# Chunk-selected attention and a soft mixture of experts: score groups regrouped, weight loads moved between pairs, first output rows stored by column halves

## The chip, the cores and the metric

The kernel runs on one core of one Trainium2 chip. Its engines work side by side and wait for each other through semaphores: TensorE (PE in the profile, its weight loads PEld), VectorE (DVE), ScalarE (ACT), GpSimd (POOL) and SyncE (SP). 16 DMA engines move data between HBM and the on-chip memory SBUF; matmuls write to PSUM. The metric is the device time of one execution in microseconds (us), as the median of several runs.

## The reference

Attention over 4 images x 8 heads, 768 positions, 64 channels a head. Each query sees 6 of 24 chunks of 32 keys, chosen by an upper bound of its scores, and within them the causal part:

```python
ub = sum(maximum(q * k_min, q * k_max), axis=-1)      # per query and chunk
ub = where(causal, ub, -1e9)
top_chunks = argsort(ub)[..., -6:]
scores = where(selected & causal, q @ k.T / 8, -1e9)
attn = softmax(scores);  x = attn @ v                 # 3072 rows x 512
```

The result goes through a soft mixture of 8 experts with 4 slots each (32 slots):

```python
logits = x @ phi                                      # 3072 x 32
slot_in = softmax(logits, over rows of all images).T @ x
slot_out[e] = relu(slot_in[e] @ w1[e]) @ w2[e]        # w1 512x1024, w2 1024x512
out = softmax(logits, over slots) @ slot_out          # 3072 x 512, float32
```

The first softmax runs over all 3072 rows, so no expert can start before the attention of all images is done.

## The kernel before

Attention goes by **pairs** of heads: 16 pairs, four to an image. The main loop (L479 to L566) is one pass for each pair i, software-pipelined by hand: the order in which the code issues instructions is the order in which each engine runs them. A pass holds the score groups of pair i (`scores`, `expo`), the chunk choice of pair i+1 (`ubound`, `select`, `ns_transposes`), the transposes of keys and queries of pair i+2, the product with v of pair i-1 (`pv`), the normalisation and transposition of pair i-2, and the loads of k and q of pair i+4 and of v of pair i+2. After every fourth pair come the steps of the experts (`moe_...`).

**Score groups.** Keys are cut into six blocks of 128, and block kg is needed by query blocks kg to 5, which makes 21 blocks of 128 x 128 for a head. `GROUPS` packs them into six groups of 384 or 512 columns. A piece (kg, q0, w, c) is key block kg against w queries from its own diagonal plus q0, put at column c. Each piece takes one score matmul (L270) and one or two mask matmuls (L280) for each head. `expo` takes one exponential on ScalarE over both heads of a group (L293), and GpSimd zeroes the upper triangle of the first 128 columns (L295). Scores live in two PSUM buffers (`p_sc`), so a group's matmuls wait for the exponential two groups earlier. Groups 0 and 1 stand at the head of the pass, 2 and 3 after the key transposes and the first part of `pv`, 4 and 5 after the query transposes.

**Weights.** Sixteen expert weights, w_sb0 to w_sb7 for w1 and w_sb8 to w_sb15 for w2 (w0 to w15 in this text), are loaded by GpSimd's DMA queue with a conversion from float32 to bfloat16, 1 MB each as written. `wplan` says how many are issued in each pass (`weights`, L473): after the loads of v (L535), in the last two passes at the head (L483). k, q and v go through the same queue.

**Tail.** After the loop the last pair is finished, the logits of the last image are reduced (L605 to L637; `keep` issues dummy matmuls), and the experts follow: `experts_in` (w1) for two halves of the hidden units, `hidden_T` transposes, `experts_out(f, gs, ys)` (w2) for hidden half f, expert groups gs (group 0 uses w8 to w11, group 1 w12 to w15) and column halves ys of the output. `so_sb` is the slots' output, scaled by `zinv` (from `zsum`). `csums` sums the row weights with 24 matmuls for `cinv`. The last loop (L737) makes 24 blocks of 128 rows, two matmuls each, scaled on VectorE and ScalarE in turn, and stores them on SP's queue, two blocks to a DMA.

Of the kernel before, what the change touches and what calls it, by code (L numbers as in the profile page):

```python
# [10 lines left out]
F32 = mybir.dt.float32  # L11
BF16 = mybir.dt.bfloat16
ALU = mybir.AluOpType
ACT = mybir.ActivationFunctionType
# [6 lines left out]
NQT = 6  # L21
P = 128
# [5 lines left out]


GROUPS = [  # L30
    [(0, 0, 384, 0)],
    [(1, 0, 256, 0), (0, 384, 128, 256)],
    [(2, 0, 512, 0)],
    [(5, 0, 128, 0), (1, 256, 384, 128)],
    [(3, 0, 384, 0)],
    [(4, 0, 256, 0), (0, 512, 256, 256)],
]
WIDTH = [sum(p[2] for p in g) for g in GROUPS]
BLOCK = {}
for _g, _pieces in enumerate(GROUPS):  # L40
    for _kg, _q0, _w, _c in _pieces:
        for _x in range(0, _w, P):
            BLOCK[(_kg, _kg + (_q0 + _x) // P)] = (_g, _c + _x)


@with_exitstack
def kernel(
# [10 lines left out]
    nc = tc.nc  # L58
    B, H = q.shape[0], q.shape[1]
    scale = 1.0 / (D ** 0.5)  # L60
    NPB = H // 2
    NPAIR = B * NPB
    Dm, NS = moe_phi.shape
    E, F = moe_w1.shape[0], moe_w1.shape[2]
    SPE = NS // E
    NDG, NFG = Dm // P, F // P
    EARLY = 14
    LAST = NPAIR - 1

    ctx.enter_context(tc.manual_schedule())  # L70
    static = ctx.enter_context(tc.tile_pool(name="static", bufs=1))


    p_sc = ctx.enter_context(tc.tile_pool(name="p_sc", bufs=2, space=PSUM))
# [12 lines left out]
    si_acc = static.tile([P, NDG + 1, NS], F32, name="si_acc")  # L87
    m_run = [static.tile([P, NS], F32, name=f"m_run{i}") for i in range(2)]
    w_sb = []
    for i in range(EARLY):  # L90
        w_sb.append(static.tile([P, NDG * F], BF16, name=f"w_sb{i}"))
    identf = static.tile([P, P], F32, name="identf")
    ones_sq = static.tile([P, P], BF16, name="ones_sq")
    NJ = NQT // 2
# [168 lines left out]
    def scores(i, g):  # L263
        ps = p_sc.tile([P, 2, 512], F32, name="sc_ps", tag="sc")
        kT, qT, nsT = st["kT", i], st["qT", i], st["nsT", i]
        for kg, q0, w, c in GROUPS[g]:
            qs = slice(kg * P + q0, kg * P + q0 + w)
            for h in range(2):
                r = slice(h * 64, (h + 1) * 64)
                nc.tensor.matmul(  # L270
                    ps[:, h, c:c + w], lhsT=kT[r, kg * P:(kg + 1) * P], rhs=qT[r, qs],
                    start=True, stop=False,
                )
            t0, t1 = kg + q0 // P, kg + (q0 + w) // P
            runs = [(x, max(t0, x * NJ), min(t1, (x + 1) * NJ)) for x in range(2)]
            runs = [r for r in runs if r[1] < r[2]]
            for x, f, l in runs:
                for h in range(2):
                    r = slice(h * 64, (h + 1) * 64)
                    nc.tensor.matmul(  # L280
                        ps[:, h, c + (f - t0) * P:c + (l - t0) * P],
                        lhsT=smask[r, x, kg].rearrange("p a b -> p (a b)"),
                        rhs=nsT[r, (f - x * NJ) * P:(l - x * NJ) * P], start=False, stop=(l == t1),
                    )
        st["scps", i, g] = ps

    def expo(i, g):
        w = WIDTH[g]
        if w == 512:
            e = ep.tile([P, 2, 512], BF16, name="e_sb", tag="e_sb")  # L290
        else:
            e = ep3.tile([P, 2, 384], BF16, name="e3_sb", tag="e3_sb")
        nc.scalar.activation(e[:, :, :w], st.pop(("scps", i, g))[:, :, :w], func=ACT.Exp, scale=scale)  # L293

        nc.gpsimd.affine_select(  # L295
            out=e[:, :, :P], in_=e[:, :, :P], compare_op=ALU.is_ge, fill=0.0,
            base=0, pattern=[[0, 2], [1, P]], channel_multiplier=-1,
        )
        st["e", i, g] = e

    def pv(i, ts):
        if i == LAST and ts[0] == 0:
            st["at", i] = p_tp.tile([P, 2, 3 * (D + 1)], F32, name="at_ps", tag="tp")
        elif i == LAST and ts[0] == 3:
            st["at", i] = p_sc.tile([P, 2, 512], F32, name="at_ps", tag="sc")
        elif ts[0] == 0:
            st["at", i] = p_at.tile([P, 2, 512], F32, name="at_ps", tag="at")
        at, tb = st["at", i], 3 if i == LAST and ts[0] > 2 else 0
        for t in ts:
            for h in range(2):  # L310
                o = at[:, h, (t - tb) * (D + 1):(t - tb + 1) * (D + 1)]
                for kg in range(t + 1):
                    g, c = BLOCK[(kg, t)]
                    nc.tensor.matmul(  # L314
                        o, lhsT=st["e", i, g][:, h, c:c + P], rhs=v_t[i % NV][:, h, kg, :],
                        start=(kg == 0), stop=(kg == t),
                    )
# [147 lines left out]
            step(i // NPB)  # L465


    wplan = {i: 1 for i in range(-1, NPAIR)}
    for i in (0, 1):
        wplan[i] = 0  # L470
    nw = 1

    def weights(i):  # L473
# [97 lines left out]
    BL = B - 1  # L571
# [12 lines left out]
    def keep(n):  # L584
        for _ in range(n):
            nc.tensor.matmul(h_ps[0][:, 1, :], lhsT=ident, rhs=w_sb[0][:, :512], start=True, stop=True)
# [22 lines left out]
    nc.tensor.matmul(pmT[:, :P], lhsT=pm, rhs=identf, is_transpose=True)  # L609
    mneg = small.tile([NS, 1], F32, name="mb", tag="mb")  # L610
    nc.vector.tensor_reduce(mneg, pmT, axis=AX.X, op=ALU.max, negate=True)
    keep(2)
    rep = identf[:NS, :NS].rearrange("p (o s) -> p o s", o=1)
    nc.tensor.matmul(
        lg2, lhsT=mneg.broadcast_to([NS, P]), rhs=rep.broadcast_to([NS, NQT, NS]), start=False, stop=True,
# [7 lines left out]
    st["d", BL] = d_sb  # L623
    rm = small.tile([P, NQT, 1], F32, name="rm", tag="rm")
    nc.vector.tensor_reduce(rm, lg1, axis=AX.X, op=ALU.max)
    dm = small.tile([P, 1, NS], F32, name="dm", tag="dm")
    nc.vector.tensor_tensor(dm[:, 0, :], m_old, bc, op=ALU.add)
    nc.scalar.activation(dm, dm, func=ACT.Exp)
# [8 lines left out]
    keep(1)  # L637
    moe_dispatch(BL)

    op = ctx.enter_context(tc.tile_pool(name="op", bufs=5))  # L640
    si = st.pop("si")
    zrow = tail.tile([1, 4, CH], F32, name="zrow")
    nc.gpsimd.memset(zrow, 1.0)
# [7 lines left out]
    for g in range(2):  # L651
# [3 lines left out]
            si_acc[:1, NDG, sl].rearrange("p (j s) -> p j s", j=4),  # L655
            si[:1, NDG, sl].rearrange("p (j s) -> p j s", j=4), op=ALU.add,
        )
    cinv = tail.tile([P, B * NQT], F32, name="cinv")
    zinv = tail.tile([P, 1], F32, name="zinv")
    cT = cT_all.rearrange("p (m a) (c x) -> p m x (a c)", a=2, x=2)  # L660

    h_sb = tail.tile([P, 2, 512], BF16, name="h_sb")
# [22 lines left out]
            i_ = hT_ps.rearrange("p a (j s) -> p a j s", j=4)[:, :, :, g * SPE:(g + 1) * SPE]  # L685
            nc.vector.tensor_copy(o, i_)

    def zsum():
        ps = p_tp.tile([P, 1], F32, name="z_ps", tag="tp")
        nc.tensor.matmul(  # L690
            ps, lhsT=zrow.rearrange("p j s -> p (j s)"), rhs=identf[:1, :1], start=True, stop=True)
        nc.vector.reciprocal(zinv, ps)

    def csums():
        ps = p_tp.tile([P, B * NQT], F32, name="cs_ps", tag="tp")
        for n in range(B * NQT):
            nc.tensor.matmul(
                ps[:, n:n + 1], lhsT=cT[:, n // 2, n % 2], rhs=ones_sq[:, :1], start=True, stop=True)
        nc.vector.reciprocal(cinv, ps)

    HD = Dm // 2
    so_t = p_at.tile([P, 2, 512], F32, name="so_ps", tag="at")
    so_ps = [so_t[:, y, :HD] for y in range(2)]

    def experts_out(f, gs, ys):
        for y, g in ((y, g) for y in ys for g in gs):
# [14 lines left out]
    hidden_T(0)  # L721
    experts_in(1, 1)
    relu(1)
    experts_out(0, [0], [0, 1])
    hidden_T(1)
    zsum()
    experts_out(0, [1], [0, 1])
    experts_out(1, [0, 1], [0])
    nc.scalar.activation(so_sb[0], so_ps[0], func=ACT.Copy, scale=zinv)
    experts_out(1, [0, 1], [1])  # L730
    nc.scalar.activation(so_sb[1], so_ps[1], func=ACT.Copy, scale=zinv)
    csums()


    homes = ((p_sc, "sc"), (p_tp, "tp"), (p_sc, "sc"), (p_tp, "tp"), (p_at, "at"))
    n = 0
    for m in range(B * NQT // 2):  # L737
        o_sb = op.tile([P, 2, Dm], F32, name="o_sb", tag="o_sb")
        rows = out[m * 2 * P:(m + 1) * 2 * P, :].rearrange("(p x) d -> p x d", x=2)
        for x in range(2):  # L740
            pool, tag = homes[n % 5]
            if n == 0:
                o_ps = pool.tile([P, 2, Dm], F32, name="o2_ps", tag=tag)
                halves = [o_ps[:, y, :HD] for y in range(2)]
            else:
                o_ps = pool.tile([P, Dm], F32, name="o_ps", tag=tag)
                halves = [o_ps[:, y * HD:(y + 1) * HD] for y in range(2)]
            for y in range(2):
                nc.tensor.matmul(halves[y], lhsT=cT[:, m, x], rhs=so_sb[y], start=True, stop=True)  # L749
            if n == 0:  # L750
                for y in range(2):
                    nc.vector.tensor_scalar_mul(o_sb[:, x, y * HD:(y + 1) * HD], halves[y], cinv[:, n:n + 1])
            elif x == 0:
                nc.vector.tensor_scalar_mul(o_sb[:, x, :], o_ps, cinv[:, n:n + 1])
            else:
                nc.scalar.activation(o_sb[:, x, :], o_ps, func=ACT.Copy, scale=cinv[:, n:n + 1])  # L756
            n += 1
            if m in (0, B * NQT // 2 - 1):
                nc.sync.dma_start(out=rows[:, x], in_=o_sb[:, x, :])
        if m not in (0, B * NQT // 2 - 1):  # L760
            nc.sync.dma_start(out=rows, in_=o_sb)


# [28 lines left out]
```

## Time and profile before

| | |
|---|---|
| median of 3 runs | 171.62 us (171.58 to 172.8) |
| the profiled execution | 172.21 us, of which its span 170.5 us |
| busy share of the span | PE 81%, DVE 71%, ACT 72%, POOL 61% |
| loads (GpSimd's queue) | 38416 packets, 26.25 MB as written |
| stores (SP's queue) | 6.29 MB |
| weight loads | 16 of 1024 KB, median 14.4 us from issue to landing |

The span runs from the first instruction to the last of one execution, and all times in the text are counted from its start. A line of the rows in order of time has start and duration in us, engine, source line, operation, written tile and read tiles, shape and number of instructions; in brackets stands the idle time of the engine just before, and who ended it. A line of the windows has the stretch, its length, busy time of PE, PEld, DVE, ACT and POOL with the number of instructions, the granted TensorE clock (1 is full speed), the DMA share and GB/s. The slices cut the span into 40 parts of 4.26 us; a digit is a share in tenths. DMA shares can pass 1, since packets overlap.

### The profile page before, as it was taken

To read this page: it belongs to the slowest core of one execution; us is meant where nothing else is said; L and a number is where in the kernel's file an instruction comes from. 1 tells how busy PE (TensorE), PEld (TensorE's weight loads), DVE (VectorE), ACT (ScalarE), POOL (GpSimd) and SP (SyncE) were. 2 spreads that over 40 slices of the span, in tenths; PEclk is the share of its full clock that TensorE was granted. 3 is DMA by queue.
4 is the path that set the end of the run, shared out by engine and by line. 5 is a ranking of instruction groups with operands and counts; after the bars stand their busy time and mean duration, and the time that the engine had idled before them with its cause. 6 is when DMAs were issued, how large, how long until landed. Compare 5 with 4: busy or idle time off the path is not lost.

```text
span 170.5 us, 6183 instructions
## 1 busy us (share of the span) xinstructions
PE 137.8 (81%) x2574; PEld 99.3 (58%) x2575; DVE 121.5 (71%) x416; ACT 122.6 (72%) x166; POOL 104.0 (61%) x202
## 2 busy tenths in 40 slices
PE   0458988999999898999999899979889989896300
PEld 0335555777666767766776667657566855763200
DVE  3468768999999976999997798988742651166510
ACT  3355999999999877999987799978777522175510
POOL 7977759788878777888878878547663800000000
PEclk9999999999999999999999999999999999999965
DMA  3999999999999999999999999999999980029995
GB/s 46 163 156 185 182 212 188 129 152 184 184 214 190 211 197 209 193 211 195 212 197 205 196 207 202 203 203 200 202 208 212 215 163 13 4 76 407 404 400 195
DMA packets 40460, 32.94 MB, mean 193 GB/s; under 512 B 26352, under 2 KB 34544, under 8 KB 40432
## 3 DMA queue, kind: packets, MB, share of 16 engines
q0 software_dynamic: 38416, 26.25, 104.2%
q1 hardware_dynamic: 2016, 6.29, 9.4%
q8 instruction: 20, 0.33, 0.7%
q14 instruction: 8, 0.07, 0.1%
HBM read 52.49 MB, written 6.29 MB: 345 GB/s over the span
## 4 chain that ended last, share of the span: by engine, by line
PE 39%; ACT 21%; DVE 15%; DMA 14%; issue 5%; POOL 2%; DVEq 0%; ACTq 0%; POOLq 0%
ACT e_sb L293 15%; DMA k_in<-in_k_dram 10%; PE sc_ps L270 7%; PE at_ps L314 5%; PE tr_ps L181 5%; PE sc_ps L280 5%; DMA out_dram<-o_sb 4%; DVE x_sb L327 3%; PE h_ps L670 2%; PE so_ps L710 2%; DVE qpn L216 2%; PE ub_ps L229 2%; DVE mx L241 2%; ACT qT L190 2%; PE xT_ps L336 2%
## 5 line engine op out<-in xcount | busy, mean ns | idle before, releaser
L293 ACT ACTIVATE e_sb<-sc_ps 128x768 bf16<-128x768 f32 (+1 forms) x96 | 82.9, 930 | 9.7 <-PE sc_ps L280 9.7
L295 POOL TENSOR_SCALAR_AFFINE_SELECT e_sb<-e_sb 128x256 bf16<-128x256 bf16 x96 | 38.7, 413 | 19.6 <-ACT e_sb L293 18.9
L270 PE MATMUL sc_ps<-qT,kT 64*128 64x384 bf16 (+3 forms) x288 | 40.3, 299 | 4.2 <-ACT e_sb L293 4.1
L280 PE MATMUL sc_ps<-nsT,smask 64*128 64x384 bf16 (+2 forms) x320 | 38.6, 281 | 0.0
L314 PE MATMUL at_ps<-v_t,e_sb 128*128 128x65 bf16 x672 | 29.8, 194 | 1.5 <-DVE x_sb L327 1.2
L314 PEld LDWEIGHTS <-e_sb 128*128 128x128 bf16 x672 | 25.3, 98 | 3.9 <-DVE x_sb L327 1.2
L270 PEld LDWEIGHTS <-kT 64*128 64x128 bf16 x288 | 17.0, 95 | 15.5 <-issue 10.4
L241 DVE MAX8 mx<-ub_ps 128x8 f32<-128x8 f32 (+1 forms) x192 | 16.9, 161 | 3.6 <-PE ub_ps L229 2.0
L280 PEld LDWEIGHTS <-smask 64*128 64x128 bf16 x320 | 16.6, 96 | 3.8 <-issue 0.6
L199 DVE TENSOR_REDUCE mm<-kT 128x24 bf16<-128x768 bf16 x16 | 15.1, 945 | 4.6 <-ACT kT L190 4.5
L190 ACT COPY kT<-tr_ps 128x768 bf16<-128x768 bf16 x16 | 12.8, 799 | 7.5 <-PE tr_ps L181 6.7
L134 POOL DMA_DIRECT2D v_t<-in_v_dram x16 | 16.7, 1045 | 2.0 <-PE ns_ps L252 1.4
L327 DVE TENSOR_TENSOR x_sb<-at_ps,inv 128x768 bf16<-128x768 f32 (+1 forms) x17 | 15.5, 911 | 0.6
L205 DVE TENSOR_REDUCE mm<-kT 128x24 bf16<-128x768 bf16 x16 | 15.1, 943 | 0.0
L181 PE MATMUL tr_ps<-ident,k_in 128*64 128x128 bf16 x192 | 9.4, 240 | 6.3 <-DMA k_in<-in_k_dram 5.5
L190 ACT COPY qT<-tr_ps 128x768 bf16<-128x768 bf16 x16 | 12.9, 805 | 2.0 <-PE tr_ps L181 2.0
L129 POOL DMA_DIRECT2D k_in<-in_k_dram x16 | 11.7, 729 | 1.5 <-POOLq L776 0.8
L122 POOL DMA_DIRECT2D w_sb<-in_moe_w_dram x16 | 11.4, 710 | 1.5 <-DMA w_sb<-in_moe_w_dram 1.5
L756 ACT ACTIVATE o_sb<-o_ps,cinv 128x512 f32<-128x512 f32 x12 | 8.1, 686 | 4.9 <-PE o_ps L749 2.4
L129 POOL DMA_DIRECT2D q_in<-in_q_dram x16 | 11.5, 720 | 0.0
L216 DVE TENSOR_SCALAR qpn<-qT 128x768 bf16<-128x768 bf16 x16 | 11.0, 685 | 0.0
L347 DVE COPY xT_sb<-xT_ps 128x768 bf16<-128x768 bf16 (+1 forms) x15 | 8.1, 540 | 4.0 <-PE xT_ps L336 3.9
(116 smaller groups left out, 196.5 us busy)
## 6 DMA issues: line engine op xcount, KB each, us to landing
w_sb<-in_moe_w_dram POOLq DMA_DIRECT2D x16, 1024.0 KB, 14.4
out_dram<-o_sb SPq DMA_DIRECT2D x10, 512.0 KB, 4.9
k_in<-in_k_dram POOLq DMA_DIRECT2D x16, 192.0 KB, 9.7
q_in<-in_q_dram POOLq DMA_DIRECT2D x16, 192.0 KB, 10.0
v_t<-in_v_dram POOLq DMA_DIRECT2D x16, 192.0 KB, 10.8
out_dram<-o_sb SPq DMA_DIRECT2D x4, 256.0 KB, 3.4
phi_sb<-in_moe_phi_dram POOLq DMA_DIRECT2D x1, 32.0 KB, 9.0
```

The costliest lines, as they stand in the source:

```text
L129: nc.gpsimd.dma_start(out=t, in_=src.rearrange("h (p g) d -> p h (g d)", p=P))
L134: nc.gpsimd.dma_start(out=v_t[i % NV][:, :, :, :D], in_=v[b, 2 * j:2 * j + 2].rearrange("h (g p) d -> p h g d", p=P),)
L181: nc.tensor.matmul(ps[h * 64:(h + 1) * 64, g, :], lhsT=src[:, h, g * D:(g + 1) * D], rhs=ident, is_transpose=True,)
L190: nc.scalar.copy(t.rearrange("d (p g) -> d p g", g=NQT), st.pop((nm + "ps", i)).rearrange("d g p -> d p g"),)
L199: nc.vector.tensor_reduce(mm[:, 0, 0, :], kT, axis=AX.X, op=ALU.min)
L241: nc.vector.max(mx[:, a, :], ub[:, a, :max(8, 4 * t + 4)])
L270: nc.tensor.matmul(ps[:, h, c:c + w], lhsT=kT[r, kg * P:(kg + 1) * P], rhs=qT[r, qs], start=True, stop=False,)
L280: nc.tensor.matmul(ps[:, h, c + (f - t0) * P:c + (l - t0) * P], lhsT=smask[r, x, kg].rearrange("p a b -> p (a b)"), rhs=nsT[r, (f - x * NJ ...
L293: nc.scalar.activation(e[:, :, :w], st.pop(("scps", i, g))[:, :, :w], func=ACT.Exp, scale=scale)
L295: nc.gpsimd.affine_select(out=e[:, :, :P], in_=e[:, :, :P], compare_op=ALU.is_ge, fill=0.0, base=0, pattern=[[0, 2], [1, P]], channel_mult ...
L314: nc.tensor.matmul(o, lhsT=st["e", i, g][:, h, c:c + P], rhs=v_t[i % NV][:, h, kg, :], start=(kg == 0), stop=(kg == t),)
L327: nc.vector.tensor_tensor(st["x", b][:, t0:t1, 2 * j:2 * j + 2, :].rearrange("p t h d -> p h t d"), at[:, :, :, :D], inv.broadcast_to([P, ...
```

## The change

`GROUPS` is repacked with the three wide groups at other places: 0 and 1 are now 512 wide, 2 and 3 are 384, 4 is 512 and 5 is 384. Group 4 holds two diagonal pieces, each with its own triangle on GpSimd, and group 5 none. The last pair has a packing of its own. `wplan` issues no weight in the passes -1, 0, 1, 3, 7 and 11, one in 2, 4, 5, 6, 8, 9, 10 and 12, two in 13, three in 14 and two in 15. The first eight weights live in a pool that is closed before the output buffers are opened. In the tail, the column sums of the first three images stand where two dummy matmuls stood, those of the last one go with the sum for `zinv`; the two halves of the slots' output have a PSUM buffer each; `experts_out` runs in another order; and the first three pairs of row blocks are computed and stored by column halves, the first halves before the experts' second half is finished.

```diff
 GROUPS = [
-    [(0, 0, 384, 0)],
-    [(1, 0, 256, 0), (0, 384, 128, 256)],
     [(2, 0, 512, 0)],
     [(5, 0, 128, 0), (1, 256, 384, 128)],
+    [(0, 0, 384, 0)],
     [(3, 0, 384, 0)],
-    [(4, 0, 256, 0), (0, 512, 256, 256)],
+    [(4, 0, 256, 0), (1, 0, 256, 256)],
+    [(0, 384, 384, 0)],
 ]
+GROUPS_LAST = [
+    [(0, 0, 512, 0)],
+    [(1, 0, 512, 0)],
+    [(2, 0, 384, 0)],
+    [(4, 0, 256, 0), (2, 384, 128, 256)],
+    [(3, 0, 384, 0), (1, 512, 128, 384)],
+    [(5, 0, 128, 0), (0, 512, 256, 128)],
+]
...
+    w_ctx = ExitStack()
+    w1p = w_ctx.enter_context(tc.tile_pool(name="w1p", bufs=1, side="right"))
     for i in range(EARLY):
-        w_sb.append(static.tile([P, NDG * F], BF16, name=f"w_sb{i}"))
+        w_sb.append((w1p if i < E else static).tile([P, NDG * F], BF16, name=f"w_sb{i}"))
...
-        nc.gpsimd.affine_select(
-            out=e[:, :, :P], in_=e[:, :, :P], compare_op=ALU.is_ge, fill=0.0,
-            base=0, pattern=[[0, 2], [1, P]], channel_multiplier=-1,
-        )
+        for kg, q0, _, c in pieces:
+            if q0 == 0:
+                nc.gpsimd.affine_select(
+                    out=e[:, :, c:c + P], in_=e[:, :, c:c + P], compare_op=ALU.is_ge, fill=0.0,
+                    base=0, pattern=[[0, 2], [1, P]], channel_multiplier=-1,
+                )
...
-    wplan = {i: 1 for i in range(-1, NPAIR)}
-    for i in (0, 1):
-        wplan[i] = 0
+    wplan = {i: 1 for i in (2, 4, 5, 6, 8, 9, 10, 12)}
+    wplan.update({13: 2, 14: 3, 15: 2})
...
-    keep(2)
...
+    def col_sums(ps, b):
+        c = cT_all[:, b * NQT:(b + 1) * NQT].rearrange("p (m a) (c x) -> p m x (a c)", a=2, x=2)
+        for n in range(NQT):
+            nc.tensor.matmul(
+                ps[:, n:n + 1], lhsT=c[:, n // 2, n % 2], rhs=ones_sq[:, :1], start=True, stop=True)
+
+    csa = p_tp.tile([P, BL * NQT], F32, name="cs_ps", tag="tp")
+    for b in range(BL):
+        col_sums(csa[:, b * NQT:(b + 1) * NQT], b)
...
     nc.vector.tensor_reduce(rm, lg1, axis=AX.X, op=ALU.max)
+    nc.vector.reciprocal(inv_a, csa)
...
-    so_t = p_at.tile([P, 2, 512], F32, name="so_ps", tag="at")
-    so_ps = [so_t[:, y, :HD] for y in range(2)]
+    so_ps = [p_at.tile([P, HD], F32, name="so_ps0", tag="at"), p_sc.tile([P, HD], F32, name="so_ps1", tag="sc")]
...
-    experts_out(0, [0], [0, 1])
+    NM, NH = B * NQT // 2, 3
...
+    def half_out(m, y):
+        o_sb = op.tile([P, 2, HD], F32, name="oh_sb", tag="oh_sb", bufs=2 * NH)
+        for x in range(2):
+            tag = next(half_homes[y])
+            o_ps = homes[tag].tile([P, HD], F32, name="oh_ps", tag=tag)
+            nc.tensor.matmul(o_ps, lhsT=cT[:, m, x], rhs=so_sb[y], start=True, stop=True)
+            scaled(x, o_sb[:, x, :], o_ps, 2 * m + x)
+            if m == y == 0:
+                nc.sync.dma_start(out=rows(m)[:, x, :HD], in_=o_sb[:, x, :])
+        if m + y > 0:
+            nc.sync.dma_start(out=rows(m)[:, :, y * HD:(y + 1) * HD], in_=o_sb)
+
+    w_ctx.close()
+    op = ctx.enter_context(tc.tile_pool(name="op", bufs=5))
+    experts_out(0, [0, 1], [0])
     hidden_T(1)
-    zsum()
-    experts_out(0, [1], [0, 1])
+    sums()
+    experts_out(0, [0], [1])
     experts_out(1, [0, 1], [0])
     nc.scalar.activation(so_sb[0], so_ps[0], func=ACT.Copy, scale=zinv)
+    experts_out(0, [1], [1])
+    half_out(0, 0)
+    half_out(1, 0)
     experts_out(1, [0, 1], [1])
     nc.scalar.activation(so_sb[1], so_ps[1], func=ACT.Copy, scale=zinv)
-    csums()
+    half_out(2, 0)
+    for m in range(NH):
+        half_out(m, 1)
...
```

`scaled` scales a block on VectorE (x = 0) or ScalarE (x = 1); `sums` makes the sum for `zinv` and the column sums of the last image with one reciprocal. Row blocks from the fourth pair on go as before.

More of the change, by code (lines that the diff above doesn't have):

```diff
@@ L30, with block_homes @@
 GROUPS = [
-    [(0, 0, 384, 0)],
-    [(1, 0, 256, 0), (0, 384, 128, 256)],
     [(2, 0, 512, 0)],
     [(5, 0, 128, 0), (1, 256, 384, 128)],
+    [(0, 0, 384, 0)],
     [(3, 0, 384, 0)],
-    [(4, 0, 256, 0), (0, 512, 256, 256)],
-]
[L38 to L43, printed above, removed]
+    [(4, 0, 256, 0), (1, 0, 256, 256)],
+    [(0, 384, 384, 0)],
+]
+GROUPS_LAST = [
[6 rows of a table added]
+]
+def block_homes(groups):
+    homes = {}
+    for g, pieces in enumerate(groups):
+        for kg, q0, w, c in pieces:
+            for x in range(0, w, P):
+                homes[(kg, kg + (q0 + x) // P)] = (g, c + x)
+    return homes
+BLOCK, BLOCK_LAST = block_homes(GROUPS), block_homes(GROUPS_LAST)
 @with_exitstack
@@ L265, in scores @@
         kT, qT, nsT = st["kT", i], st["qT", i], st["nsT", i]
-        for kg, q0, w, c in GROUPS[g]:
+        for kg, q0, w, c in (GROUPS_LAST if i == LAST else GROUPS)[g]:
             qs = slice(kg * P + q0, kg * P + q0 + w)
@@ L287, in expo @@
     def expo(i, g):
-        w = WIDTH[g]
+        pieces = (GROUPS_LAST if i == LAST else GROUPS)[g]
+        w = sum(x[2] for x in pieces)
         if w == 512:
@@ L312, in pv @@
                 for kg in range(t + 1):
-                    g, c = BLOCK[(kg, t)]
+                    g, c = (BLOCK_LAST if i == LAST else BLOCK)[(kg, t)]
                     nc.tensor.matmul(
@@ L611, with cinv @@
     nc.vector.tensor_reduce(mneg, pmT, axis=AX.X, op=ALU.max, negate=True)
-    keep(2)
+    inv_a = tail.tile([P, BL * NQT], F32, name="inv_a")
+    inv_b = tail.tile([P, 1 + NQT], F32, name="inv_b")
+    def cinv(n):
+        return inv_a[:, n:n + 1] if n < BL * NQT else inv_b[:, 1 + n - BL * NQT:2 + n - BL * NQT]
+    def col_sums(ps, b):
[6 more added lines that the diff above has]
+        col_sums(csa[:, b * NQT:(b + 1) * NQT], b)
     rep = identf[:NS, :NS].rearrange("p (o s) -> p o s", o=1)
@@ L638 @@
     moe_dispatch(BL)
-    op = ctx.enter_context(tc.tile_pool(name="op", bufs=5))
     si = st.pop("si")
@@ L657 @@
         )
-    cinv = tail.tile([P, B * NQT], F32, name="cinv")
-    zinv = tail.tile([P, 1], F32, name="zinv")
+    zinv = inv_b[:, :1]
     cT = cT_all.rearrange("p (m a) (c x) -> p m x (a c)", a=2, x=2)
@@ L686, in hidden_T, with sums @@
             nc.vector.tensor_copy(o, i_)
-    def zsum():
-        ps = p_tp.tile([P, 1], F32, name="z_ps", tag="tp")
+    def sums():
+        ps = p_tp.tile([P, 1 + NQT], F32, name="z_ps", tag="tp")
         nc.tensor.matmul(
[L691 to L699, printed above, removed]
+            ps[:, :1], lhsT=zrow.rearrange("p j s -> p (j s)"), rhs=identf[:1, :1], start=True, stop=True)
+        col_sums(ps[:, 1:], BL)
+        nc.vector.reciprocal(inv_b, ps)
     HD = Dm // 2
-    so_t = p_at.tile([P, 2, 512], F32, name="so_ps", tag="at")
-    so_ps = [so_t[:, y, :HD] for y in range(2)]
+    so_ps = [p_at.tile([P, HD], F32, name="so_ps0", tag="at"), p_sc.tile([P, HD], F32, name="so_ps1", tag="sc")]
     def experts_out(f, gs, ys):
@@ L723, with rows, scaled @@
     relu(1)
-    experts_out(0, [0], [0, 1])
+    NM, NH = B * NQT // 2, 3
+    homes = {"sc": p_sc, "tp": p_tp, "at": p_at}
+    half_homes = [iter("tp at sc tp tp at".split()), iter("sc tp sc tp at tp".split())]
+    def rows(m):
+        return out[m * 2 * P:(m + 1) * 2 * P, :].rearrange("(p x) d -> p x d", x=2)
+    def scaled(x, o, ps, n):
+        if x == 0:
+            nc.vector.tensor_scalar_mul(o, ps, cinv(n))
+        else:
+            nc.scalar.activation(o, ps, func=ACT.Copy, scale=cinv(n))
@@ L735 @@
-    homes = ((p_sc, "sc"), (p_tp, "tp"), (p_sc, "sc"), (p_tp, "tp"), (p_at, "at"))
+    half_out(2, 0)
+    for m in range(NH):
+        half_out(m, 1)
     n = 0
-    for m in range(B * NQT // 2):
+    for m in range(NH, NM):
         o_sb = op.tile([P, 2, Dm], F32, name="o_sb", tag="o_sb")
-        rows = out[m * 2 * P:(m + 1) * 2 * P, :].rearrange("(p x) d -> p x d", x=2)
         for x in range(2):
[L741 to L747, printed above, removed]
-            for y in range(2):
[L749 to L756, printed above, removed]
@@ L757 @@
+            tag = ("sc", "tp", "sc", "tp", "at")[n % 5]
+            o_ps = homes[tag].tile([P, Dm], F32, name="o_ps", tag=tag)
+            for y in range(2):
+                nc.tensor.matmul(
+                    o_ps[:, y * HD:(y + 1) * HD], lhsT=cT[:, m, x], rhs=so_sb[y], start=True, stop=True)
+            scaled(x, o_sb[:, x, :], o_ps, 2 * m + x)
             n += 1
[L758 to L761, printed above, removed]
+            if m == NM - 1:
+                nc.sync.dma_start(out=rows(m)[:, x], in_=o_sb[:, x, :])
@@ L765 @@
+        if m < NM - 1:
+            nc.sync.dma_start(out=rows(m), in_=o_sb)
 _INS = ['q', 'k', 'v', 'moe_phi', 'moe_w1', 'moe_w2']
```

## The prediction

> **What bounds the kernel now.** I read the slices first, then the windows, then rows in order of time. The slices' last two lines, DMA and GB/s:
>
> ```profile
> DMA  3999999999999999999999999999999980029995
> GB/s 46 163 156 185 182 212 188 129 152 184 184 214 190 211 197 209 193 211 195 212 197 205 196 207 202 203 203 200 202 208 212 215 163 13 4 76 407 404 400 195
> ```
>
> The loads keep the DMA engines at nine tenths from the second slice to about 137 us and then stop. There is a hole of some 10 us, and the output follows at 400 GB/s. So there are two limits one behind the other: a loop whose loads never rest, and an output as fast as the DMA writes. The windows show three stages (us; PE, PEld, DVE, ACT, POOL busy; clock; DMA share; GB/s): an ordinary pair of 6.87 us, a stretch in which only weights move, and the output.
>
> ```profile
> 36.29:43.16 6.87, 6.55 (x127) 4.73 (x127) 6.46 (x23) 6.53 (x9) 5.84 (x12) 1.00 1.25 171
> 130.00:136.00 6.00, 5.78 (x137) 4.71 (x136) 3.32 (x8) 4.40 (x6) 3.86 (x6) 1.00 1.07 215
> 152.70:168.30 15.60, 4.79 (x33) 2.86 (x30) 6.82 (x10) 6.21 (x10) 0.00 (x0) 0.85 1.02 400
> ```
>
> In a pair, VectorE (6.46) and ScalarE (6.53) have some 0.4 us to spare, most of it one wait of VectorE and a few of ScalarE for scores. In the second row a weight of 1.049 MB takes 1.049/215 = 4.9 us. Sixteen take 78 us; that is why the DMA is full, and why a late weight can't be hurried.
>
> **Part 1, the score groups.** Before, exponentials 0 and 1 are 384 wide (829 ns each) and cover less of TensorE's stretch of second score group, bound, key transposes, PV and third group than two of 512 (1031 ns) will. The third then waits for TensorE (0.23 us at 38.84), all later ones are late by it, and VectorE waits for the mask transposes:
>
> ```profile
> 41.20 0.26 DVE L207 TENSOR_TENSOR bd<-mm,headsel 128x96 bf16<-128x96 bf16 x1
> 41.76 0.36 DVE L260 COPY nsT<-ns_ps 128x384 bf16<-128x384 bf16 x1 [0.30 <-PE ns_ps L252]
> ```
>
> With the wide groups ahead, ScalarE has 0.4 us more before the third exponential, and 0.4 us less after it. Its waits and the 0.30 us can go; VectorE is then late next, full at 6.86 - 0.30 = 6.56 us. Gain: 0.30 us for a pair. Pairs 1 to 12 lie before the point that counts below: 12 x 0.30 = 3.6, less something for the pairs with expert work (8.3 to 9 us, with other waits), plus the one wait for a key load in the loop (0.69 us at 112.72). I take G = 3.5 us; bounds 0 (VectorE and POOL give nothing) and 6 (half of ScalarE's idle time from 15.7 to 121 us, 12 us by windows). Two score and two mask matmuls a pair fewer: the columns stay 2688 a head, and pitch goes by columns (0.11 us for a pair of 256), so nothing. The masks of POOL stay 6 a pair (413 ns), two now behind one exponential; PV of that pair starts over 1 us later, so nothing. The last pair has four more mask matmuls (0.1 us) and orders its groups for its PV: covered by part 2, else within 0.5 us either way.
>
> **Part 2, the weights.** Nine (w0 to w8) are issued up to pair 12, and w9 to w15 in pairs 13 (two), 14 (three), 15 (two). The loads of k, q, v are the same, so in four pairs three weights instead of four share the DMA: it gets pauses, and what it doesn't carry then comes at the end. POOL's rows at the end of pair 13 and the start of 14:
>
> ```profile
> 116.80 1.03 POOL L134 DMA_DIRECT2D v_t<-in_v_dram  x1
> 117.83 0.70 POOL L122 DMA_DIRECT2D w_sb<-in_moe_w_dram  x1
> 118.53 0.81 POOL L295 TENSOR_SCALAR_AFFINE_SELECT e_sb<-e_sb 128x256 bf16<-128x256 bf16 x2
> 119.29 0.72 POOL L122 DMA_DIRECT2D w_sb<-in_moe_w_dram  x1
> ```
>
> These two issues are w13 and w14 now; at 117.83 - G it will be w9, behind v of pair 15. Allowing 1.7 us from issue to first byte (an estimate; the quickest load of 0.2 MB landed 3.5 us after issue), w9 flows from 119.5 - G. Seven weights one after the other take 7 x 4.9 = 34.3 us. Now w15, issued at 125.95, flows at full rate to 136.5 and lands near 143, since some DMA engines finish late; with a shorter saturated stretch I allow 2 us. So w15 lands at X = 119.5 - 3.5 + 34.3 + 2 = 152.3.
>
> Who needs it: the new order puts all of w8 to w15 into the first block of expert outputs (half 0 of the hidden, groups 0 and 1), and TensorE goes in order. Today that block starts here:
>
> ```profile
> 144.42 1.05 PE L710 MATMUL so_ps<-w_sb,hT_pad 128*32 128x256 bf16 x32
> 145.40 0.41 PE L682 MATMUL hT_ps<-ident,h_sb 128*128 128x128 bf16 x4
> ```
>
> Sixteen matmuls later, at 144.9 - G - 0.6 (pairs 13 to 15 gain 0.6), about 140.8, it needs w15. **TensorE waits some 11 us** with everything queued behind it: second hidden transposes, sums, all expert outputs, all output. This holds at any G, since G moves both ends: what decides is issue time plus 34 us.
>
> Moved with the weights: POOL issues 2.1 us at the start of pair 14 instead of 0.72, 1.4 instead of 0.77 in 15, 0.7 more in 13. Behind them stand masks, the mask cast and the max subtraction (L394) that ScalarE's exponential needs; up to 2 us late in pairs 14 and 15. The 11 us hide that; without them it costs 1 to 2. In the trace the loads take eight semaphores in turn, and POOL waits for the load eight before (1.5 us in all, three times now); w8, eight before w15, has long landed. The new home of w0 to w7 and the output buffers laid over it cost nothing: their last readers, the experts' first layer, end before the first output is written.
>
> **Part 3, the tail**, from X. Now 32 matmuls take 0.97 us of pitch (64 in 1.93), so at full clock: 16 (0.49) + transposes 0.35 + sums (0.31 + 6 x 0.031) + 16 (0.49) + 32 (0.97) = 2.8; ScalarE's copy to so_sb 0.52; two matmuls, VectorE 0.48 and the issue 0.9. First store at X + 4.2. Now the stores begin at 151.73 and the span ends 18.8 us later, paced by the DMA. That stays: 6.29 MB either way. Six stores of 1 KB rows: 2 KB packets take 84 ns, 4 KB 164, so 1 KB about 44 on that line, 6% slower for 1.57 MB: 0.25 us. A gap before the second halves: 0.5 us. End = X + 4.2 + 18.8 + 0.75 = X + 23.7. Without a late weight X would be 144.9, the end 168.6: the tail alone is worth 1.9 us (the 0.58 us wait for the shared so_ps and 0.6 us of column sums leave the path, and stores begin before the second half). The 18 column sums that replace two dummy matmuls take 18 x 0.031 = 0.56 us against 0.59, before a wait for VectorE that ends no sooner; the added reciprocal (0.31) falls into 0.63 us of VectorE idle. Nothing, 0.3 at worst.
>
> **The clock.** TensorE was slow until 20.3 us, and at the end the granted clock is 0.50 in the last 2.2 us, with the last matmul at 161.3. The same pair of 256 columns follows the one before in 0.21 us early, 0.10 us later:
>
> ```profile
> 13.95 0.42 PE L270 MATMUL sc_ps<-qT,kT 64*128 64x256 bf16 x2
> 14.16 0.42 PE L280 MATMUL sc_ps<-nsT,smask 64*128 64x256 bf16 x2
> ...
> 20.42 0.27 PE L280 MATMUL sc_ps<-nsT,smask 64*128 64x256 bf16 x2
> 20.52 0.27 PE L270 MATMUL sc_ps<-qT,kT 64*128 64x256 bf16 x2
> ```
>
> Dense work from 12.55 us took until 20.3 to reach full speed. After 11 us of idling I take the slow speed for the 2.8 us: between +0 and +2.8, I take +2.4. The Trainium skill, "TensorE: Matmul & The Clock Gate", Part 1, says the same against this change: after an idle window of about 3.4 us the clock is halved until a window of sustained work has passed. By it the stretch costs 2.4 to 2.8 us more; the rows agree.
>
> **Sum.** Span 152.3 + 23.7 + 2.4 = 178.4, against 170.5: +7.9. The profiled execution took 172.21 (span and 1.71 around it), 0.59 over the median; I add the 7.9 to the median: **179.5 us**.
>
> **Rivals.**
> - *Late weights, full clock* (18%): the wait counts as short or partly filled. 177.1.
> - *Late weights, loop gains nothing* (10%): POOL's longer queue or VectorE eats G. 179.5 + 3.5 = 183.0.
> - *The weights are in time* (5%), the other side: then loop (4.1) and tail (1.9) count, 171.6 - 6.0 = 165.6. It decides at (144.9 - 0.6 - 119.5 - 2)/7 = 3.3 us a weight, so 320 GB/s. Against it: no slice of the loop passes 215 GB/s. The Trainium skill, "DMA: Bandwidth & Descriptors", Specifications, gives a ceiling of 435 GB/s; the loads read float32, twice what they write, so 430 GB/s read: at it already.
> - *About even* (5%): G = 6 or more, landing without tail, full clock: X = 147.8, end 171.5; some 172.6.
> - Forecast: 62%. All of it slower: the change doing what it says in its first and third parts is worth 6 us, and the second takes them and more.
>
> The range takes G from 0 to 6, tail 0 to 3 and both clocks, cut to 8 in 10: 175.5 to 183.5. About 1% is what a measurement here tells from no change. Faster by over 1%: 0.05; within: 0.05; slower: 0.90.
>
> **What would show it.** Right: ordinary pairs of 6.5 to 6.6 us without the wait before nsT; DMA digits under 9 in the loop, then solid to 150; TensorE idle some 11 us from about 141 in so_ps, released by the DMA of w_sb; clock 0.5 there; stores from about 159. Wrong: weights landing faster than 4 us each, or pairs so short that w9 is issued before 108.

## The result and the profile after

The changed kernel takes 180.5 us (median of 4 runs, 179.46 to 180.98) against 171.83 us: ratio 1.0485, 95% interval 1.042 to 1.055. It is slower by 8.7 us. The prediction was 179.5 us in a range of 175.5 to 183.5. The medians and ratios from here on leave out executions over 1.5% slower than the fastest of the same kernel: two of six in one experiment and three of ten in another.

The profiled execution has a span of 179.0 us (170.5 before). Its slices, clock, DMA and GB/s:

```profile
PEclk9999999999999999999999999999996965589855
DMA  3999999999999999999999999999999995029994
GB/s 51 167 156 181 188 84 129 115 181 184 128 196 189 216 191 209 180 173 206 174 205 198 202 84 201 168 192 215 212 216 218 210 217 110 4 75 358 404 403 168
```

The loads now pause in the loop (84, 129, 115 and 128 GB/s, and again 84), and then run at 210 to 218 GB/s up to slice 33. The slices' digits hide the pauses; the DMA digits from 20 to 60 us in steps of 1 us, after and before, show them:

```profile
DMA  9999804999904999999999999999699899999999
DMA  9999999999999699999999999999999999999999
```

The hole before the output is still there, but the loads end some 9 us later. The windows, in the columns of the prediction: an ordinary pair, then the experts' first layer, the wait, the restart, and the stores.

```profile
42.33:48.80 6.47, 6.38 (x124) 4.50 (x122) 6.21 (x22) 6.43 (x9) 5.57 (x11) 1.00 1.32 150
134.00:140.00 6.00, 5.63 (x78) 2.48 (x78) 1.27 (x7) 0.69 (x2) 0.00 (x0) 0.72 1.08 217
140.00:150.00 10.00, 1.90 (x35) 0.84 (x28) 0.07 (x1) 0.60 (x1) 0.00 (x0) 0.73 1.02 206
150.00:156.00 6.00, 4.12 (x61) 3.00 (x64) 0.49 (x3) 0.00 (x0) 0.00 (x0) 0.50 0.07 14
164.00:176.00 12.00, 2.70 (x17) 1.40 (x15) 4.00 (x6) 3.60 (x6) 0.00 (x0) 0.69 1.02 400
```

A pair is 0.40 us shorter (6.87 before), and ScalarE is busy for 6.43 of its 6.47 us. Between 140 and 150 us the engines all but rest (TensorE is busy for 1.90 us) and weights move at 206 GB/s. TensorE's rows in order of time show the wait itself:

```profile
140.55 0.71 PE L734 MATMUL so_ps<-w_sb,hT_pad 128*32 128x256 bf16 x17
142.11 0.27 PE L734 MATMUL so_ps<-w_sb,hT_pad 128*32 128x256 bf16 x1 [0.85 <-DMA w_sb<-in_moe_w_dram]
146.99 0.37 PE L734 MATMUL so_ps<-w_sb,hT_pad 128*32 128x256 bf16 x1 [4.61 <-DMA w_sb<-in_moe_w_dram]
151.88 1.01 PE L734 MATMUL so_ps<-w_sb,hT_pad 128*32 128x256 bf16 x13 [4.52 <-DMA w_sb<-in_moe_w_dram]
152.82 0.61 PE L713 MATMUL hT_ps<-ident,h_sb 128*128 128x128 bf16 x4
153.37 0.58 PE L721 MATMUL z_ps<-identf,zrow 1*128 1x1 f32 x2
153.88 0.32 PE L639 MATMUL z_ps<-ones_sq,cT_all 128*128 128x1 bf16 x6
154.13 3.61 PE L734 MATMUL so_ps<-w_sb,hT_pad 128*32 128x256 bf16 x64
```

Sixteen matmuls of group 0 run, then one matmul for each weight that lands: w12 was there, w13 at 142.1, w14 at 147.0, w15 at 151.9, 4.9 us apart. The last row is the clock: 64 matmuls in 3.61 us, where they took 1.93 before:

```profile
146.05 1.93 PE L710 MATMUL so_ps<-w_sb,hT_pad 128*32 128x256 bf16 x64
```

The whole difference of the spans can be read at one point, the first need of w15. Before, TensorE got there at 146.05; now at 141.0, which is 5.05 us earlier. It leaves at 151.88, 10.9 us later. From there to the end it took 24.4 us before (170.47 - 146.05) and takes 27.1 now. So -5.05 + 10.9 + 2.7 = +8.5 us.

### The profile page after: what moved, and what is told of

It is laid out like the page before. It is cut to its first block, busy times and chain, and to the rows that moved or that the text cites. A ratio compares the mean times of both kernels' runs of the same rounds, so it can differ in the third digit from the quotient of the medians.

```text
span 179.0 us, 6067 instructions
## 1 busy us (share of the span) xinstructions
PE 139.9 (78%) x2516; PEld 97.6 (55%) x2517; DVE 120.9 (68%) x418; ACT 122.0 (68%) x169; POOL 103.4 (58%) x202
## 4 chain that ended last, share of the span: by engine, by line
ACT 24%; DMA 22%; DVE 19%; PE 19%; POOL 6%; issue 5%; SPq 0%; DVEq 0%; POOLq 0%; ACTq 0%
DMA w_sb<-in_moe_w_dram 17%; ACT e_sb L310 14%; ACT kT L206 3%; PE sc_ps L286 3%; PE so_ps L734 3%; DVE mx L257 3%; DVE mm L215 3%; DVE mm L221 3%; DMA out_dram<-o_sb 3%; ACT qT L206 3%; PE sc_ps L296 2%; DVE qpn L232 2%; POOL w_sb L138 2%; POOL e_sb L314 2%; PE tr_ps L197 2%
## 5 line engine op out<-in xcount | busy, mean ns | idle before, releaser
L310 ACT ACTIVATE e_sb<-sc_ps 128x1024 bf16<-128x1024 f32 (+1 forms) x96 | 83.1, 921 | 7.0 <-PE sc_ps L296 6.7
L286 PE MATMUL sc_ps<-qT,kT 64*128 64x384 bf16 (+3 forms) x258 | 37.7, 312 | 1.8 <-ACT e_sb L310 0.8
L286 PEld LDWEIGHTS <-kT 64*128 64x128 bf16 x258 | 14.2, 95 | 9.4 <-issue 4.6
L150 POOL DMA_DIRECT2D v_t<-in_v_dram x16 | 17.2, 1078 | 1.0 <-PE ns_ps L268 0.8
L296 PEld LDWEIGHTS <-smask 64*128 64x128 bf16 x294 | 15.1, 96 | 4.0 <-issue 0.6
L734 PE MATMUL so_ps<-w_sb,hT_pad 128*32 128x256 bf16 x128 | 7.0, 361 | 10.0 <-DMA w_sb<-in_moe_w_dram 10.0
L780 ACT ACTIVATE so_sb<-so_ps,inv_b 128x256 bf16<-128x256 f32 x1 | 0.5, 474 | 15.6 <-PE so_ps L734 15.6
L734 PEld LDWEIGHTS <-hT_pad 128*32 128x32 bf16 x128 | 4.4, 123 | 12.0 <-issue 11.0
```

The source lines that it names most:

```text
L150: nc.gpsimd.dma_start(out=v_t[i % NV][:, :, :, :D], in_=v[b, 2 * j:2 * j + 2].rearrange("h (g p) d -> p h g d", p=P),)
L286: nc.tensor.matmul(ps[:, h, c:c + w], lhsT=kT[r, kg * P:(kg + 1) * P], rhs=qT[r, qs], start=True, stop=False,)
L296: nc.tensor.matmul(ps[:, h, c + (f - t0) * P:c + (l - t0) * P], lhsT=smask[r, x, kg].rearrange("p a b -> p (a b)"), rhs=nsT[r, (f - x * NJ ...
L734: nc.tensor.matmul(so_ps[y][j * CH:(j + 1) * CH, :], lhsT=hT_pad[:, fg, e, :], rhs=w_sb[E + e][:, fg * Dm + y * HD:fg * Dm + (y + 1) * HD] ...
```

## The experiments

Ten kernels, each timed beside the kernel before. The first four ask whether the weights carry the whole loss, and what the clock costs.

**Changed kernel, old weight plan.**

```diff
-    wplan = {i: 1 for i in (2, 4, 5, 6, 8, 9, 10, 12)}
-    wplan.update({13: 2, 14: 3, 15: 2})
+    wplan = {i: 1 for i in range(-1, NPAIR)}
+    for i in (0, 1):
+        wplan[i] = 0
```

> The changed kernel with the weight plan of before (one weight a pair, none in pairs 0 and 1); groups and tail stay changed. Theory (the late weights are the whole loss): w15 lands near 143 us instead of 151.9 and TensorE's 10 us wait in so_ps is gone. But the loads then never rest, so k of the last pair lands near 112 us as before, 5 us after the faster loop wants it; the loop loses most of its gain there. Some 168 us, ratio to before 0.98. Rival (groups or tail carry the loss): 173 us or more, with the first expert outputs not waiting for a DMA.

Measured 170.02 us, ratio 0.986 (0.979 to 0.993), 2 us above the expected 168. The wait in so_ps is gone: 32 matmuls in a row, then the next block.

```profile
144.18 1.05 PE L735 MATMUL so_ps<-w_sb,hT_pad 128*32 128x256 bf16 x32
146.04 1.93 PE L735 MATMUL so_ps<-w_sb,hT_pad 128*32 128x256 bf16 x64
```

But these stand almost at the times of the kernel before (144.42 and 146.05): the loop's 5 us are gone too. The waits of this run between 60 and 130 us (waiting engine and line, releaser; us in all, times, longest):

```profile
POOL w_sb L138 <- DMA w_sb<-in_moe_w_dram: 6.8, 4, 2.8
PE tr_ps L197 <- DMA k_in<-in_k_dram: 4.6, 4, 1.7
```

TensorE waits 4.6 us for keys, as expected. The other row was not expected: GpSimd stands 6.8 us in front of weight issues, until an earlier weight has landed.

**Kernel before, new weight plan alone.** The edit is the one above, turned round, in the kernel before.

> The kernel before with the new weight plan alone. Theory: w9 is issued at 117.8 us, seven weights take 34.3, w15 lands at 155.8; what followed its first use at 146.05 took 24.45 us to the end, and 3 us come on top for the slow clock: span 183, some 184.4 us, slower than the whole change. Rival (the plan is harmless, groups or tail do it): 171 to 173 us.

Measured 184.74 us, ratio 1.072 (1.066 to 1.078), and w15 is waited for until 157.0:

```profile
157.03 3.34 PE L709 MATMUL so_ps<-w_sb,hT_pad 128*32 128x256 bf16 x61 [4.51 <-DMA w_sb<-in_moe_w_dram]
```

So the plan alone loses more than the whole change. With the run before, the weights' move is the cause and neither groups nor tail.

**One weight moved instead of seven, out of pair 10.** To the old plan:

```diff
+    wplan[10], wplan[13] = 0, 2
```

> The changed kernel with the plan of before but for one weight moved from pair 10 to pair 13. Theory: one weight fewer ahead of k of the last pair brings that load 4.9 us earlier, so the loop keeps its 6.5 us pairs, and the DMA still never rests, so w15 lands near 142.5, 2 us after TensorE is ready for it. End 142.5 + 23.7 = 166.2, some 167.3 us, ratio 0.974, a little under the run with the whole old plan. Rival (the groups gain nothing once the DMA is full): the same as that run or more.

Measured 167.77 us, ratio 0.972 (0.966 to 0.978). The time is as expected, but not by the expected way: the loop lost 2.8 us in passes 9 and 10, and w15 (its packets end at 139.7) bound nothing. GpSimd's rows show the start of that loss:

```profile
81.81 1.19 POOL L150 DMA_DIRECT2D v_t<-in_v_dram  x1 [0.43 <-PE ns_ps L268]
85.73 0.70 POOL L138 DMA_DIRECT2D w_sb<-in_moe_w_dram  x1 [2.73 <-DMA w_sb<-in_moe_w_dram]
```

In the trace the loads take eight semaphores in turn, so an issue waits for the landing of the load eight before it (here a weight issued at 69.39, landed at 85.42); with four loads to a pair that is the weight of two pairs ago. Once the queue is two pairs long, GpSimd stops with all masks behind it. TensorE then waited 1.8 us for k, and the granted clock fell to 0.5 (from 87.0 to 93.8 us in the clock's record).

**Dummy work in the wait.** In the changed kernel, between groups 0 and 1:

```diff
-    experts_out(0, [0, 1], [0])
+    experts_out(0, [0], [0])
+    warm = p_tp.tile([P, 512], F32, name="warm_ps", tag="tp")
+    for _ in range(50):
+        nc.tensor.matmul(warm, lhsT=ident, rhs=w_sb[E][:, :512], start=True, stop=True)
+    experts_out(0, [1], [0])
```

> The changed kernel with 50 dummy matmuls of 512 columns (10.7 us) between the expert outputs of group 0 and those of group 1, where TensorE waits for weights. Theory (the clock falls in the wait and costs 2.4 us): the stretch after the landing of w15 runs at full clock, the first store comes 2 to 2.5 us earlier, some 178.2 us. Rival (the output's DMA or the landing sets the end whatever the clock is): 180.5 us as the change. If the dummies end after the landing they add up to 0.5 us.

Measured 179.63 us, 0.9 us less than the change (ratios to before 1.041 and 1.0485, with overlapping intervals). TensorE's and SP's rows:

```profile
140.73 10.96 PE L778 MATMUL warm_ps<-w_sb,ident 128*128 128x512 bf16 x49
151.63 0.29 PE L734 MATMUL so_ps<-w_sb,hT_pad 128*32 128x256 bf16 x3
153.09 0.60 PE L734 MATMUL so_ps<-w_sb,hT_pad 128*32 128x256 bf16 x13 [1.18 <-DMA w_sb<-in_moe_w_dram]
...
154.51 1.93 PE L734 MATMUL so_ps<-w_sb,hT_pad 128*32 128x256 bf16 x64
...
157.45 0.85 SPq L769 DMA_DIRECT2D out_dram<-oh_sb  x2
```

(One of the 50 dummies has no record.) The 64 matmuls take 1.93 us again. From the last weight to the first store it is 157.45 - 153.09 = 4.36 us; in the changed kernel (first store at 158.67) it is 6.79. So the clock costs 2.4 us. Only 0.9 us of it is seen in the time. In this profile w15 landed 1.2 us later, and from the first store to the end it took 21.0 us instead of 20.3. The dummies did not cause the late landing: w9, issued at the same time in both (112.1), already landed at 123.6 instead of 122.5, 17 us before the first dummy. So landings differ by that much between executions, and what the clock is worth in the whole time is not measured finely here.

The next four separate groups, tail and the length of the queue.

**The weight taken out of pair 6 instead of 10.** `wplan[6], wplan[13] = 0, 2` on the old plan, in the changed kernel.

> The changed kernel with the plan of before, but the weight of pair 6 moved to pair 13. With the weight moved out of pair 10 the loads' queue had grown so long by pair 9 that GpSimd stood 2.7 us in front of a weight's issue, until the load eight before it had landed, and the clock fell after it. Theory: taking the weight out earlier keeps the queue some 5 us shorter, that wait and the one for k of pair 12 go, pairs stay at 6.5 us to the end, and the landing of w15 near 140.5 sets the first store (145). Span 165 to 165.5, some 166.7 us, 1 us less than with pair 10. Rival (the loop's 2.8 us come back in full): 165.0 us. Rival (the queue is as long): 167.8 us.

Measured 167.7 us, ratio 0.976 (0.972 to 0.980). GpSimd's wait and the waits for k are gone: k of the last pair is transposed at 107.8 us, near the changed kernel's 107.5, against 110.3 with pair 10. But the first store comes at 145.5, hardly before the 145.8 with pair 10, because now w15 is last (TensorE waits for it until 141.1). The loop's gain meets the DMA's floor, and the times can't be told apart. The time is the one the second rival gave, 1 us above the theory's, but not for the rival's reason: the queue did get shorter.

**Two dummy matmuls put back.** The same kernel with `keep(2)` ahead of the column sums.

> The same with two dummy matmuls of 512 columns put back ahead of the 18 column sums. In the changed kernel the clock fell to 0.5 for 3.4 us right behind these sums (134.4), and the experts' first layer took 5.7 us instead of 4.3. Theory (18 matmuls of one column count as idling for the clock, two of 512 don't): no 0.5 between 130 and 140, first layer 4.3 us; 0.4 us of dummies against 1.4 us; if w15 doesn't bind, 1 us less than without them, at best 165.7, if it does, the same. Rival (the fall has to do with the phase of the clock's window, not with these matmuls): it stays in the trace and the run is 0.4 us slower.

Measured 167.03 us, ratio 0.974 (0.969 to 0.978). The fall of the clock in the first layer is gone and the layer takes 4.3 us instead of 5.6, but the time is the same within its interval, as w15 binds. On the cause it is not conclusive. In the profiles of the seven kernels with the 18 sums and no dummies, the clock fell by the first layer in five. Of the five kernels with two dummies it fell in one, the kernel of the next experiment (from 136.0). But four of these five have the old tail, without the 18 sums, so this run alone has both. That the dummies help is likely; it is not shown, and what decides between kernels with the same code stays open.

**Groups alone.** Kernel before with the new `GROUPS`, `GROUPS_LAST` and masks.

> The kernel before with the new score groups alone (old plan, old tail). Theory (the old plan keeps the DMA full, so the loop can't be faster than its loads): pairs of 6.5 us up to pair 9, then waits for k, k of the last pair transposed near 112 as before; gain 1 to 2 us, some 170.3 us, ratio 0.99. Rival (the groups' gain is their own, whatever the loads do): 4 to 6 us, 166 to 168 us.

Measured 169.6 us, ratio 0.988 (0.983 to 0.993). The waits between 60 and 130 us:

```profile
POOL w_sb L136 <- DMA w_sb<-in_moe_w_dram: 2.5, 2, 2.1
PE tr_ps L195 <- DMA k_in<-in_k_dram: 1.7, 2, 1.0
```

Two us and not five: with the old plan the faster loop runs into its own loads. The clock fell in this run too, for 3.4 us from 88.2 and again from 136.0 us, so the waits need not be all that it lost.

**New groups, pair 6's weight moved, old tail.**

> New groups, the plan with pair 6 moved to 13, but the tail of before (order of the expert outputs, sums and whole-row stores). From the first use of w15 the old tail took 25.8 us with its plan late, the new one 27.1; undisturbed, the old one 24.4 and the new one, with the 20.3 us it takes from its first store, 24.5. Theory (the new tail gives back after its first store what it gains before it): within 0.7 us of the run with the new tail, 166 to 167.3 us. Rival (the new tail is worth the 1.9 us of the prediction): 168.5 us.

Measured 167.3 us, ratio 0.974 (0.970 to 0.978), the same as with the new tail (0.976). From w15's release to the end the old tail takes 24.45 us (141.07 to 165.52) and the new one 24.7 (141.12 to 165.80). The new tail's first store is 1.2 us earlier, and its stores take 20.3 us from the first issue instead of 18.8. So with w15 last the new tail is worth nothing. Where w15 is not last it is worth about 1 us: from the first expert output to the end, the kernels with the old plan and with pair 10's weight moved take 25.1 us (144.18 to 169.30, 140.95 to 166.06), the kernel before 26.05 (144.42 to 170.47).

The last two ask for the slope.

**One weight of the changed plan moved earlier**, from pair 14 to pair 7.

```diff
-    wplan = {i: 1 for i in (2, 4, 5, 6, 8, 9, 10, 12)}
-    wplan.update({13: 2, 14: 3, 15: 2})
+    wplan = {i: 1 for i in (2, 4, 5, 6, 7, 8, 9, 10, 12)}
+    wplan.update({13: 2, 14: 2, 15: 2})
```

> The changed kernel with one weight moved from pair 14 to pair 7, where the DMA has a pause; six weights instead of seven behind pair 13. Theory (w15 lands at issue time plus 4.9 us a weight, TensorE waits for it): landing at 147, TensorE idle 5 us instead of 10, the clock still falls, first store 153.8, span 174, some 175.2 us; 172.8 if the clock stays up. Rival (the loss comes of the crowd of issues on GpSimd in pairs 13 to 15): within 1 us of the change.

Measured 175.93 us, ratio 1.022 (1.014 to 1.030): 4.6 us less for one weight than the changed kernel. The row of the landing, 3.5 us earlier and not the 4.9 of the theory:

```profile
148.41 1.01 PE L734 MATMUL so_ps<-w_sb,hT_pad 128*32 128x256 bf16 x13 [4.51 <-DMA w_sb<-in_moe_w_dram]
```

TensorE now also waits 0.9 us for k of the last pair (not at all in the changed kernel).

**A second one**, to pair 3 (one in each of pairs 2 to 10, 12 and 13, two in 14 and 15).

> The same with a second weight moved, to pair 3: five behind pair 13. Theory: landing at 142, TensorE ready at 141, wait about 1 us, too short for the clock; first store 146.5, 20.3 us from there, some 168 us: the slope ends here, since from this point TensorE and not the DMA is last. Rival (the slope goes on, 4.9 us a weight below the level of the plan with one weight out of pair 6): 166 us or less.

Measured 171.9 us, ratio 0.999 (0.995 to 1.004), 4 us above what was expected. Its rows: the wait for k in the loop, the landing of w15, and the 64 matmuls behind it.

```profile
PE tr_ps L197 <- DMA k_in<-in_k_dram: 3.1, 3, 1.6
144.47 0.60 PE L734 MATMUL so_ps<-w_sb,hT_pad 128*32 128x256 bf16 x13 [1.45 <-DMA w_sb<-in_moe_w_dram]
145.89 3.10 PE L734 MATMUL so_ps<-w_sb,hT_pad 128*32 128x256 bf16 x64
```

With a weight in each of nine pairs running, the loop waits for k again (3.1 us), and the last weights are issued that much later. The clock was at 0.5 twice for 3.4 us (from 136.2 and from 146.5), once in the first layer and once in these 64 matmuls. The slope went on at 4.0 us for this weight, and w15 is still last, so its end was not reached at the fifth weight. A guess that no run tests alone: the end lies where the DMA has no pause at all. The plan with pair 6 has its first weight in pass -1 and so uses the pause before pair 2, which this plan leaves empty.

## Why the prediction was right, step by step

- **What bounds.** Right. The loads fill the DMA, a weight takes 4.9 us whoever waits (142.11, 146.99, 151.88), and no run hurried it. Of the signs named, the pauses did not show as digits under 9 in the slices, only in GB/s and in digits of 1 us; the pairs (6.47 us), the wait from 141 us, the clock of 0.5 and the first store (158.67) came as named.
- **Part 1, the term G.** Mis-sized: 3.5 us predicted, 5.7 measured (w9 is issued at 112.10 instead of 117.83). Two pieces of it. A pair is 6.47 us, not 6.56: the floor was put at VectorE's rows, but those overlap a little, and the engine that filled up was ScalarE (6.43 of 6.47). So ordinary pairs gained 0.4 us each; those with expert work gained 0.1 to 0.3, and the last stretch before the issue, with the wait for k (0.69), gained 1.6.
- **Part 2, w15's landing.** 152.3 predicted, 151.9 measured, but two errors cancel. The issue came 2.2 us earlier than taken, and from issue to landing it took 39.8 us (112.10 to 151.88) instead of 38.0 (117.8 to 155.8). The seven weights land 4.9 us apart, as predicted, so the missing 1.8 us all lie in the first: w9 landed at 122.5, 10.4 us after its issue, where the prediction's terms give 1.7 + 4.9 + 2 = 8.6. The prediction also misread the kernel before a little: its loads kept the full rate (213 GB/s) to 138 us and not to 136.5.
- **TensorE's wait.** 11 us predicted from 140.8; it stands from 141.0 to 151.9 and is idle 10.0 of that. That both ends of the wait move with G was right: with the plan alone, without the groups' gain, TensorE stood as long (145.9 to 157.0). The time does move with G: that run took 184.74 us.
- **The clock.** +2.4 us predicted, 2.4 measured (6.79 against 4.36 us, from w15's release to the first store). The Trainium skill, "TensorE: Matmul & The Clock Gate", Part 1, has the clock halved after an idle window of about 3.4 us; the 10 us wait agrees, at 0.50 from 150 to 156 us, while the fall after a wait of 1.8 us in one run is not covered by an idle window of that length.
- **Part 3, the tail.** Mis-sized: 18.8 + 0.75 us from the first store to the end, 20.3 measured (20.3 in six of the eight kernels with the new tail, 20.5 and 21.0 in the two others). The 1 KB packets took 47 ns and not 44, and the first seven stores start with a gap (162 GB/s from 160.6 to 161.2 us, then 343). X + 4.2 to the first store was 4.36 at full clock; the listed steps give it only without the issue's 0.9 us, which already lies in the 18.8. The sum at full clock is X + 24.7, not 23.7. So "the tail alone is worth 1.9 us" fell: it is worth about 1 us where w15 is not last, and nothing where it is.
- **The sum.** Span 178.4 predicted, 179.0 measured: w15's landing came 0.4 us early, the tail took 1.0 longer. The mechanism is the predicted one; that the number is so close is in part luck, since G and the time from issue to landing were each off by about 2 us in opposite directions.
- **The sentence that groups and tail are worth 6 us** was the largest error, though it changed nothing in the sum. With the old plan the groups give 2 us, where GpSimd and TensorE wait for loads; groups and one moved weight together give 4, with either tail. What moving that weight is worth with the old groups was not run. Given the new groups, moving one weight gained 2 us; moving seven lost 10.
- **GpSimd's crowd of issues** in pairs 13 to 15 was covered, as predicted; the rule that an issue waits for the eighth load before it did no harm there. It did in the loop of the old plan once the pairs were shorter: 6.8 us, where the prediction had only the 1.5 us of the kernel before.

A version that beats both kernels came out of it: new groups, the old plan with pair 6's weight moved to pair 13, old tail, 167.3 us, ratio 0.974 to the kernel before.

## What to carry to other kernels

Where a transfer queue is full from end to end, moving a load later is free only if the queue stays full in the meantime: every pause that the new plan leaves is paid at the end, here 4.6 and 4.0 us for the two weights that were moved back. Find the first instruction that needs the last load, and compare issue time plus queue with the time at which its engine gets there; work saved elsewhere only makes that wait longer. And a loop that gets faster needs its loads earlier: look how much lead the prefetch has left before counting the gain.

## What the runs showed of the hardware that was not expected

- GpSimd stood up to 2.8 us in front of a load's issue, until an earlier load had landed (6.8 us in one run), with all its other work behind it.
- The granted clock fell to 0.5 for 3.4 us just before or in the experts' first layer in six of twelve kernels; the same code had the fall in one kernel and not in another. In the middle of the dense loop it fell for 6.8 us after a wait of 1.8 us in one kernel, and for 3.4 us after two waits of 0.7 us in another (the groups alone), while a wait of 1.7 us in a third (the changed kernel with the old plan) left it at full.
- Stores of 1 KB rows took 47 ns a packet, those of 2 KB 84 and of 4 KB 165.
